# Attention, experts and soft experts on one core: operand sums on VectorE, and expert 0's second products one group later

## The chip, the cores and the metric

One core of a Trainium2 chip. The time is device time in microseconds of one execution. The engines are TensorE (PE in the rows; its weight loads are PEld), VectorE (DVE), ScalarE (ACT), GpSimd (POOL) and SyncE (SP), whose queue issues most DMAs.

## The reference

```python
# attention over q, k, v (4 batches, 8 heads, 576 positions, 64 wide), causal window of 128, ALiBi bias
scores = np.where(mask, scores + bias, -1e9)
attn = softmax(scores); attn_out = attn @ v
x = attn_out.transpose(0, 2, 1, 3).reshape(2304, 512)
# dense mixture: all 4 experts on all tokens, weighted by probabilities
for e in range(4):
    h = np.maximum(x @ w1[e], 0.0)          # 512 -> 1024
    out += p[:, e:e+1] * (h @ w2[e])        # 1024 -> 512
# soft mixture: 8 experts of 4 slots, on softmax-weighted sums of all tokens
logits = out @ phi
slot_input = softmax_over_tokens(logits).T @ out
slot_out[e] = np.maximum(slot_input[e] @ m1[e], 0.0) @ m2[e]
result = softmax_over_slots(logits) @ slot_out
```

## The kernel before

Every product is made in 16-bit parts: an operand is split in a high and a low half (`hi`, `lo`), and three products of halves are added in PSUM. Tokens come in 18 tiles of 128.

**Attention with expert 0 between (up to some 285 us).** The loop in lines 436 to 483 goes over 72 steps, four a tile, each for a pair of heads. Step n makes the scores (`qk`, lines 322 to 336), the softmax (`soft`, lines 338 to 362: VectorE adds the bias and finds the extreme, ScalarE takes exp and the high half, GpSimd the low half at line 358, and a transposing DMA of SP's queue, line 293, makes `eT`), and then the product with v (`pv`, lines 364 to 376) of an earlier step: `LAG` = 2 steps back (line 419; one step for the first tile). `eT` has five buffers (line 360). After a tile's four `pv`, `xn` and `xn_c` normalise it and transpose it to `xT`.

Between the steps, pieces of expert 0 are put in with a budget of 2000 estimated ns a step (line 476). A group is one tile of tokens for the first four, then two. Its pieces (`moe_pieces`, lines 243 to 257) are eight first products (`l1_piece`, L206, one for each 128 columns of the hidden layer, then ScalarE's relu at L214 and VectorE's low half at L215) and after them, for each tile, two halves of the second product (`l2_mm`, L228), the second of which ends with VectorE's L236. First products use two PSUM banks, second products two others. A hidden tile `h` holds two blocks of up to 512 tokens in one of 23 slabs that `acc`, the weights, staged loads and `ct` share. Pieces that the budget leaves over come after the loop (lines 667 to 675), with the jobs of the next stage between.

**Seven-product stage (some 346 to 751 us).** Experts 1, 2 and half of 3 are worked off in 10 quarters (`QS`), each with three groups of six tiles, 30 units. The first products of a unit (`unit_l1`, matmuls at L566) are seven products of sums of operands in place of eight plain ones; the second products (`unit_l2`, L641) of the unit before stand between them, with VectorE's L238 adding each to `acc`. The sums of x are made once for each of the three groups by `xsum_jobs` (lines 500 to 538): eight 128x768 sums at L507 on GpSimd, then ScalarE's L510 and VectorE's L511 for the halves of four results. The sums of weights are made for each quarter by `w7_jobs` (lines 540 to 558): four 128x256 sums at L550 on GpSimd, then L554 and L555. The temporaries of both and the units' `h` share three buffers (`h6`). All three groups' x sums are made ahead of the stage.

**Then** the rest of expert 3, with the soft mixture, and the output.

The code's order sets priorities only: the program is built with a scheduler that goes by a simulated timeline (`schedule_with_timeline_sim=True`), and that may put an instruction which is ready ahead of ones that stand before it. What it fixed is the order on each engine, which the trace shows.

Of the kernel before, what the change touches and what calls it, by code (L numbers as in the profile page):

```python
# [9 lines left out]
F16 = mybir.dt.float16  # L10
BF16 = mybir.dt.bfloat16
AF = mybir.ActivationFunctionType
ALU = mybir.AluOpType
# [6 lines left out]
def kernel(  # L20
# [13 lines left out]
    nc = tc.nc  # L34
    P = 128
# [6 lines left out]
    FC = F // P  # L42
# [27 lines left out]
    def sl(shape, dt, name, pool=None):  # L70
        return (pool or slab).tile(shape, dt, tag="slab", name=nm(name))
# [129 lines left out]
    def l1_piece(e, t0, n, fc, key):  # L201
        pt = ps.tile([P, 512], F32, tag="L1", name=nm("l1"))[:, 0:n]
        first_mm = True
        for kc in range(KC):
            for wa, xa in ((0, 0), (0, 1), (1, 0)):
                nc.tensor.matmul(pt, lhsT=w1_ap(e, fc, wa, kc), rhs=x_ap(t0, n, xa, kc),  # L206
                                 start=first_mm, stop=(kc == KC - 1 and wa == 1))
                first_mm = False
        kk = (key, fc // 2)
        if kk not in hh:  # L210
            hh[kk] = sl([P, 2, 2, 512], F16, "h") if e < 3 else h3[h3n[0] % 2].rearrange("p (a b c) -> p a b c", a=2, b=2)
            h3n[0] += e == 3
        ht = hh[kk][:, fc % 2, :, 0:n]
        nc.scalar.activation(out=ht[:, 0], in_=pt, func=AF.Relu)  # L214
        nc.vector.scalar_tensor_tensor(out=ht[:, 1], in0=pt, scalar=0.0, in1=ht[:, 0],  # L215
                                       op0=ALU.max, op1=ALU.subtract)
# [4 lines left out]
    def l2_mm(e, t, o, fcs, key, lo, hi):  # L221
        if lo == 0:
            l2p[key, t] = ps2.tile([P, 512], F32, tag="L2", name=nm("l2"))
        pt = l2p[key, t]
        for fc in fcs[lo:hi]:
            ht = hh[key, fc // 2]
            for ha, wa in ((0, 0), (0, 1), (1, 0)):
                nc.tensor.matmul(pt, lhsT=ht[:, fc % 2, ha, o:o + P], rhs=w2_ap(e, fc, wa),  # L228
                                 start=(fc == fcs[0] and ha == 0 and wa == 0),
                                 stop=(fc == fcs[-1] and ha == 1))  # L230

# [106 lines left out]
    def soft(i, hp, st):  # L338
# [18 lines left out]
        nc.scalar.activation(out=e2[:, :, 0], in_=et[:, :, c0:], func=AF.Copy)  # L357
        nc.gpsimd.tensor_tensor(out=e2[:, :, 1], in0=et[:, :, c0:], in1=e2[:, :, 0], op=ALU.subtract)  # L358
        nb = 4 * w // P
        eTt = at([P, 8, P], F16, "eT", 5)  # L360
        trans(eTt[:, 0:nb], e2.rearrange("p a b c -> p (a b c)"), nb, i < 2)
        eT[i, hp] = eTt

# [52 lines left out]
    swap_q(0)  # L416
    sp_v_hi(0)
    sp_v_lo(0)
    LAG = 2
    NS = NT * 4  # L420
    PE_T = 2

# [8 lines left out]
    for tl in groups0:  # L431
        avail.append((pvt(4 * tl[-1] + 3) + (3 if tl[-1] else 1), tl))
    pend = []
    wq = [(0, qd, j) for a in (0, 2) for qd in range(4) for j in (a, a + 1)]
    budget = 0.0
    for n in range(NS + LAG + 3):
# [35 lines left out]
        while avail and avail[0][0] <= n:  # L472
            tl = avail.pop(0)[1]
            alloc_acc(tl[0])
            pend += moe_pieces(0, tl, list(range(FC)), True)
        budget = min(budget + 2000.0, 5000.0)
        while pend and budget > 0:
            c, f = pend.pop(0)
# [21 lines left out]
    def xsum_jobs(sg):  # L500
# [3 lines left out]
            return st[i // 2][:, i % 2].rearrange("p k (i t) -> p k i t", t=P)  # L504

        def tt(o, x, y, op):
            nc.gpsimd.tensor_tensor(out=o, in0=x, in1=y, op=op)  # L507

        def out(b, i):
            nc.scalar.activation(out=XS[sg][:, b, 0], in_=st[i // 2][:, i % 2], func=AF.Copy)  # L510
# [29 lines left out]
    def w7_jobs(e, qd):  # L540
        t = {}

        def j0():
            W7[e, qd] = sub.tile([P, 7, 2, 2, P], F16, tag="w7", name=nm("w7"), bufs=2)
            t[0] = h6([P, 4, 2, P], F32, "wt")
            sa = stg[e, qd, 0].rearrange("p (b k) (z f) -> p b k z f", b=2, z=2)
            t[1] = sa
            for o, x, y in ((t[0][:, 0], sa[:, 0, :, 1], sa[:, 0, :, 0]), (t[0][:, 1], sa[:, 1, :, 1], t[0][:, 0]),
                            (t[0][:, 2], sa[:, 1, :, 1], sa[:, 0, :, 1]), (t[0][:, 3], sa[:, 1, :, 0], t[0][:, 1])):
                nc.gpsimd.tensor_tensor(out=o, in0=x, in1=y, op=ALU.subtract)  # L550

        def sp(a, b, src):
            d = W7[e, qd]
            nc.scalar.activation(out=d[:, a:b, 0], in_=src, func=AF.Copy, scale=WS)  # L554
            nc.vector.scalar_tensor_tensor(out=d[:, a:b, 1], in0=src, scalar=WS, in1=d[:, a:b, 0],  # L555
                                           op0=ALU.mult, op1=ALU.subtract)
        return [j0, lambda: sp(0, 2, t[1][:, :, :, 0]), lambda: sp(2, 3, t[1][:, 1:2, :, 1]),
                lambda: sp(3, 7, t[0])]
# [88 lines left out]
    while avail:  # L647
        tl = avail.pop(0)[1]
        alloc_acc(tl[0])
        pend += moe_pieces(0, tl, list(range(FC)), True)  # L650
    QS = [(e, qd) for e in (1, 2) for qd in range(4)] + [(3, 0), (3, 1)]
    QP = [(3, 2), (3, 3)]
    QA = QS + QP
# [1 line left out]
    def qjobs(x):  # L655
# [8 lines left out]
                r += [lambda j=j: split_w(e, qd, j) for j in (0, 1)]  # L664
            r += [lambda j=j: split_w(e, qd, j) for j in (2, 3)]
        return r
    jobs = [lambda: load_w(*QA[0])] + qjobs(0) + [j for sg in range(NSG) for j in xsum_jobs(sg)]
    per = -(-len(jobs) // max(1, len(pend)))
    while pend:
        for _ in range(per):  # L670
# [2 lines left out]
        pend.pop(0)[1]()  # L673
    for jb in jobs:
        jb()
    hh.clear()


    prev = []
    for x, (e, qd) in enumerate(QS):  # L680
        jobs = qjobs(x + 1) + (qjobs(x + 2) if x == len(QS) - 1 else [])
        for sg in range(NSG):
            u, L = unit_l1(e, qd, sg)
            order = [L[0], 0, L[1], L[2], 0, L[3], L[4], 0, 0, L[5], 0, L[6], 0]
# [9 lines left out]
            jb()  # L694
    for f in prev:
        f()
    sums_pool.__exit__(None, None, None)
    slb = ctx.enter_context(tc.tile_pool(name="slb", bufs=17))

# [337 lines left out]
```

## Time and profile before

| | us |
|---|---|
| runs (3), median | 954.52 |
| lowest, highest | 953.16, 954.74 |
| profiled execution | 952.59 |
| its span, first to last instruction | 950.8 |
| TensorE busy in the span | 883.7 |
| VectorE, ScalarE, GpSimd busy | 559.0, 372.4, 269.7 |

The profile is of one execution. A row of grouped instructions names the line, the engine, the operation, the tiles (written <- read), the shape, the count, the busy time in us and the mean of one in ns. A row of waits reads: engine and line that waited <- what ended the wait: us in total, how many times, the longest. PEclk is the granted share of TensorE's clock: 1.00 is 2.4 GHz, 0.50 is 1.2 GHz. Waits of PE and PEld for the same thing overlap and are not to be added.

### The profile page before, as it was taken

The numbers are of one execution on the slowest core, as the hardware profiler recorded it, in microseconds if no ns is written. First come the engines' busy times: TensorE is split into PE (matmuls) and PEld (weight loads), VectorE is DVE, ScalarE is ACT, GpSimd is POOL, SyncE is SP. The second block draws the span as 40 slices with busy tenths as digits, with TensorE's granted clock in tenths as the row PEclk, the third lists the DMA queues.
The fourth block names the chain that finished last, engine by engine and source line by source line (L and its number), as shares of the span: only waits on it lengthen the run. The fifth ranks groups of instructions, "written<-read, shape, count | busy, mean of one in ns | idle before, by whom it ended". The sixth has DMA issues, their size and how long they took to land.

```text
span 950.8 us, 16499 instructions
## 1 busy us (share of the span) xinstructions
PE 883.7 (93%) x6514; PEld 514.7 (54%) x6514; DVE 559.0 (59%) x1170; ACT 372.4 (39%) x920; POOL 269.7 (28%) x240
## 2 busy tenths in 40 slices
PE   3589999899899989999999999999999999999797
PEld 2467766566675545555555555555555445554432
DVE  9965545546538586666565747566657464456612
ACT  5787647767633343323232313232323101222412
POOL 7766536556528940101010110101010004410000
PEclk9999999999999999999999999999999999999799
DMA  9599988999870110100001010101001007983796
GB/s 262 113 184 178 204 142 151 176 187 193 138 148 22 45 45 1 45 15 30 23 23 45 1 45 1 45 1 45 18 28 45 1 1 291 223 217 116 240 385 235
DMA packets 222030, 102.37 MB, mean 108 GB/s; under 512 B 187216, under 2 KB 201584, under 8 KB 221952
## 3 DMA queue, kind: packets, MB, share of 16 engines
q1 hardware_dynamic: 212320, 78.14, 39.1%
q10 hardware_dynamic: 6800, 13.11, 3.9%
q0 software_dynamic: 2832, 10.07, 2.9%
q8 instruction: 51, 0.84, 0.4%
q14 instruction: 27, 0.22, 0.1%
HBM read 64.59 MB, written 4.72 MB: 73 GB/s over the span
## 4 chain that ended last, share of the span: by engine, by line
PE 71%; DMA 9%; POOL 6%; ACT 5%; DVE 4%; issue 3%; SPq 2%; POOLq 0%; ACTq 0%; DVEq 0%
PE l L641 25%; PE A L566 12%; PE l L228 8%; PE l L206 8%; PE C L566 6%; DMA eT<-e 4%; PE B L566 3%; POOL st L507 3%; DMA kT<-ks 2%; DMA qT<-qs 2%; PE hp L969 2%; ACT e L352 1%; PE so_ps L987 1%; PE x L375 1%; PE fp L1000 1%
## 5 line engine op out<-in xcount | busy, mean ns | idle before, releaser
L641 PE MATMUL l<-w,h 128*128 128x512 f16 x1080 | 253.0, 379 | 0.0
L238 DVE SCALAR_TENSOR_TENSOR acc<-l,pr,acc 128x512 f32<-128x512 f32 x216 | 161.5, 749 | 134.2 <-PE l L641 110.8
L566 PEld LDWEIGHTS <-w 128*128 128x128 f16 x1260 | 123.6, 98 | 100.1 <-issue 3.5
L228 PE MATMUL l<-w,h 128*128 128x512 f16 x648 | 161.5, 382 | 8.1 <-ACT h L214 7.0
L641 PEld LDWEIGHTS <-h 128*128 128x128 f16 x1080 | 105.7, 98 | 115.2
L206 PE MATMUL l<-xT,w 128*128 128x256 f16 (+2 forms) x1344 | 162.9, 272 | 4.7 <-DVE h L215 3.9
L206 PEld LDWEIGHTS <-w 128*128 128x128 f16 x1344 | 116.8, 99 | 42.1 <-issue 6.5
L590 ACT ACTIVATE ct<-A 128x384 f32<-128x384 f32 x90 | 43.5, 488 | 219.4 <-PE A L566 219.3
L550 POOL TENSOR_TENSOR wt<-stg 128x256 f32<-128x256 f32 x20 | 14.5, 746 | 336.7 <-PE l L641 297.3
L358 POOL TENSOR_TENSOR e<-e,e 128x512 f16<-128x512 f32 (+1 forms) x72 | 80.7, 1125 | 69.8 <-ACT e L357 49.6
L228 PEld LDWEIGHTS <-h 128*128 128x128 f16 x648 | 60.2, 99 | 63.9 <-ACT h L214 7.8
L214 ACT ACTIVATE h<-l 128x256 f16<-128x256 f32 (+2 forms) x112 | 40.2, 366 | 104.5 <-PE l L206 67.2
L352 ACT ACTIVATE e<-e,nmx 128x256 f32<-128x256 f32 (+1 forms) x144 | 69.7, 485 | 24.6 <-DVE nmx L347 24.4
L215 DVE SCALAR_TENSOR_TENSOR h<-l,h 128x256 f16<-128x256 f32 (+2 forms) x112 | 44.9, 409 | 51.0 <-ACT h L214 50.2
L566 PE MATMUL C<-xs,w 128*128 128x384 f16 x360 | 72.2, 326 | 0.0
L566 PE MATMUL A<-xs,w 128*128 128x384 f16 x360 | 70.7, 329 | 1.0 <-ACT ct L590 1.0
L347 DVE CUSTOM_DVE_ANT_0 e<-s,bias 128x256 f32<-128x256 f32 (+1 forms) x144 | 52.8, 404 | 26.2 <-PE s L335 14.7
L566 PE MATMUL A<-xT,w 128*128 128x384 f16 x360 | 67.6, 326 | 0.6 <-ACT ct L590 0.6
L585 ACT ACTIVATE h<-ct 128x384 f16<-128x384 f32 x90 | 44.0, 515 | 43.8 <-PE l L641 31.6
L593 DVE TENSOR_TENSOR ct<-ct,C 128x384 f32<-128x384 f32 x60 | 33.1, 551 | 36.1 <-ACT ct L590 26.1
L375 PE MATMUL x<-vv,eT 128*128 128x64 f16 x816 | 40.0, 197 | 14.7 <-DMA eT<-e 10.1
L330 PE MATMUL s<-kT,qT 128*128 128x128 f16 x272 | 46.3, 230 | 6.9 <-DVE qT L299 2.5
(181 smaller groups left out, 1040.9 us busy)
## 6 DMA issues: line engine op xcount, KB each, us to landing
m<-in_moe_w_dram ACTq DMA_DIRECT2D x25, 512.0 KB, 5.3
stg<-in_moe_w_dram SPq DMA_DIRECT2D x20, 512.0 KB, 4.6
m<-in_moe_w_dram SPq DMA_DIRECT2D x20, 512.0 KB, 10.2
m<-in_moe_w_dram POOLq DMA_DIRECT2D x19, 512.0 KB, 11.8
stg<-in_moe_w_dram SPq DMA_DIRECT2D x24, 256.0 KB, 3.2
out_dram<-ots SPq DMA_DIRECT2D x18, 256.0 KB, 3.4
qr<-in_q_dram SPq DMA_DIRECT2D x16, 256.0 KB, 4.5
kr<-in_k_dram SPq DMA_DIRECT2D x16, 256.0 KB, 4.0
```

The costliest lines, as they stand in the source:

```text
L206: nc.tensor.matmul(pt, lhsT=w1_ap(e, fc, wa, kc), rhs=x_ap(t0, n, xa, kc), start=first_mm, stop=(kc == KC - 1 and wa == 1))
L215: nc.vector.scalar_tensor_tensor(out=ht[:, 1], in0=pt, scalar=0.0, in1=ht[:, 0], op0=ALU.max, op1=ALU.subtract)
L228: nc.tensor.matmul(pt, lhsT=ht[:, fc % 2, ha, o:o + P], rhs=w2_ap(e, fc, wa), start=(fc == fcs[0] and ha == 0 and wa == 0), stop=(fc == fc ...
L238: nc.vector.scalar_tensor_tensor(out=a, in0=pt, scalar=p, in1=a, op0=ALU.mult, op1=ALU.add)
L330: nc.tensor.matmul(o, lhsT=qT[i][:, 0, h], rhs=mv, start=True, stop=False)
L347: nc.vector.tensor_tensor_reduce(out=et[:, hl, c0:], in0=st[:, hl, c0:], in1=bias[:, h, c0:], op0=ALU.add, op1=ALU.min, scale=-0.125, scal ...
L352: nc.scalar.activation(out=et[:, hl, c0:], in_=et[:, hl, c0:], func=AF.Exp, scale=-1.0, bias=nmx[i][:, h:h + 1], accum_out=sums[i][:, h:h ...
L358: nc.gpsimd.tensor_tensor(out=e2[:, :, 1], in0=et[:, :, c0:], in1=e2[:, :, 0], op=ALU.subtract)
L375: nc.tensor.matmul(o, lhsT=t[:, (hl * 2 + ea) * nk + kb - kb0], rhs=vvs[i - 1 + kb][:, h, va], start=(kb == kb0 and ea == 0 and va == 0), ...
L566: nc.tensor.matmul(o, lhsT=wq_[:, blk, wa, kc], rhs=xf(xa, kc), start=(first and kc == 0 and wa == 0 and xa == 0), stop=(kc == 1 and wa == 1),
L585: nc.scalar.activation(out=o[:, 0], in_=src, func=AF.Relu)
L641: nc.tensor.matmul(pt, lhsT=u["h"][:, z, ha, par, i * P:(i + 1) * P], rhs=w2_ap(e, 2 * qd + z, wa), start=(z == 0 and ha == 0 and wa == 0) ...
```

## The change

It does five things. The x sums (L507) and the weight sums (L550) are issued on VectorE instead of GpSimd. The third group's x sums move from ahead of the seven-product stage into its first quarter, and the first group's come before the first quarter's weight jobs. Expert 0's second products of one group are queued between the first products of the next (`queue_moe0`), the last group's last three pieces between the first products of the stage's first unit (`tail0`). Expert 0's hidden tiles hold four blocks of 256 tokens instead of two of 512. `LAG` goes from 2 to 3 and `eT` from five buffers to six.

```diff
--- before.py
+++ after.py
@@ -206,11 +206,17 @@
                 nc.tensor.matmul(pt, lhsT=w1_ap(e, fc, wa, kc), rhs=x_ap(t0, n, xa, kc),
                                  start=first_mm, stop=(kc == KC - 1 and wa == 1))
                 first_mm = False
-        kk = (key, fc // 2)
-        if kk not in hh:
-            hh[kk] = sl([P, 2, 2, 512], F16, "h") if e < 3 else h3[h3n[0] % 2].rearrange("p (a b c) -> p a b c", a=2, b=2)
-            h3n[0] += e == 3
-        ht = hh[kk][:, fc % 2, :, 0:n]
+        if e == 0:
+            kk = (key, fc // 4)
+            if kk not in hh:
+                hh[kk] = sl([P, 4, 2, 256], F16, "h")
+            ht = hh[kk][:, fc % 4, :, 0:n]
+        else:
+            kk = (key, fc // 2)
+            if kk not in hh:
+                hh[kk] = h3[h3n[0] % 2].rearrange("p (a b c) -> p a b c", a=2, b=2)
+                h3n[0] += 1
+            ht = hh[kk][:, fc % 2, :, 0:n]
         nc.scalar.activation(out=ht[:, 0], in_=pt, func=AF.Relu)
         nc.vector.scalar_tensor_tensor(out=ht[:, 1], in0=pt, scalar=0.0, in1=ht[:, 0],
                                        op0=ALU.max, op1=ALU.subtract)
@@ -223,9 +229,9 @@
             l2p[key, t] = ps2.tile([P, 512], F32, tag="L2", name=nm("l2"))
         pt = l2p[key, t]
         for fc in fcs[lo:hi]:
-            ht = hh[key, fc // 2]
+            ht = hh[key, fc // 4][:, fc % 4] if e == 0 else hh[key, fc // 2][:, fc % 2]
             for ha, wa in ((0, 0), (0, 1), (1, 0)):
-                nc.tensor.matmul(pt, lhsT=ht[:, fc % 2, ha, o:o + P], rhs=w2_ap(e, fc, wa),
+                nc.tensor.matmul(pt, lhsT=ht[:, ha, o:o + P], rhs=w2_ap(e, fc, wa),
                                  start=(fc == fcs[0] and ha == 0 and wa == 0),
                                  stop=(fc == fcs[-1] and ha == 1))
 
@@ -357,7 +363,7 @@
         nc.scalar.activation(out=e2[:, :, 0], in_=et[:, :, c0:], func=AF.Copy)
         nc.gpsimd.tensor_tensor(out=e2[:, :, 1], in0=et[:, :, c0:], in1=e2[:, :, 0], op=ALU.subtract)
         nb = 4 * w // P
-        eTt = at([P, 8, P], F16, "eT", 5)
+        eTt = at([P, 8, P], F16, "eT", 6)
         trans(eTt[:, 0:nb], e2.rearrange("p a b c -> p (a b c)"), nb, i < 2)
         eT[i, hp] = eTt
 
@@ -416,7 +422,7 @@
     swap_q(0)
     sp_v_hi(0)
     sp_v_lo(0)
-    LAG = 2
+    LAG = 3
     NS = NT * 4
     PE_T = 2
 
@@ -431,6 +437,19 @@
     for tl in groups0:
         avail.append((pvt(4 * tl[-1] + 3) + (3 if tl[-1] else 1), tl))
     pend = []
+    late = []
+
+    def queue_moe0(tl):
+        pcs = moe_pieces(0, tl, list(range(FC)), True)
+        l1, l2 = pcs[:FC], pcs[FC:]
+        per_l2 = max(1, len(l1) // max(1, len(late)))
+        for n, pc in enumerate(l1):
+            pend.append(pc)
+            if late and (n + 1) % per_l2 == 0:
+                pend.append(late.pop(0))
+        pend.extend(late)
+        late[:] = l2
+
     wq = [(0, qd, j) for a in (0, 2) for qd in range(4) for j in (a, a + 1)]
     budget = 0.0
     for n in range(NS + LAG + 3):
@@ -472,7 +491,7 @@
         while avail and avail[0][0] <= n:
             tl = avail.pop(0)[1]
             alloc_acc(tl[0])
-            pend += moe_pieces(0, tl, list(range(FC)), True)
+            queue_moe0(tl)
         budget = min(budget + 2000.0, 5000.0)
         while pend and budget > 0:
             c, f = pend.pop(0)
@@ -504,7 +523,7 @@
             return st[i // 2][:, i % 2].rearrange("p k (i t) -> p k i t", t=P)
 
         def tt(o, x, y, op):
-            nc.gpsimd.tensor_tensor(out=o, in0=x, in1=y, op=op)
+            nc.vector.tensor_tensor(out=o, in0=x, in1=y, op=op)
 
         def out(b, i):
             nc.scalar.activation(out=XS[sg][:, b, 0], in_=st[i // 2][:, i % 2], func=AF.Copy)
@@ -547,7 +566,7 @@
             t[1] = sa
             for o, x, y in ((t[0][:, 0], sa[:, 0, :, 1], sa[:, 0, :, 0]), (t[0][:, 1], sa[:, 1, :, 1], t[0][:, 0]),
                             (t[0][:, 2], sa[:, 1, :, 1], sa[:, 0, :, 1]), (t[0][:, 3], sa[:, 1, :, 0], t[0][:, 1])):
-                nc.gpsimd.tensor_tensor(out=o, in0=x, in1=y, op=ALU.subtract)
+                nc.vector.tensor_tensor(out=o, in0=x, in1=y, op=ALU.subtract)
 
         def sp(a, b, src):
             d = W7[e, qd]
@@ -647,7 +666,9 @@
     while avail:
         tl = avail.pop(0)[1]
         alloc_acc(tl[0])
-        pend += moe_pieces(0, tl, list(range(FC)), True)
+        queue_moe0(tl)
+    pend += late[:-3]
+    tail0 = [f for c, f in late[-3:]]
     QS = [(e, qd) for e in (1, 2) for qd in range(4)] + [(3, 0), (3, 1)]
     QP = [(3, 2), (3, 3)]
     QA = QS + QP
@@ -664,7 +685,8 @@
                 r += [lambda j=j: split_w(e, qd, j) for j in (0, 1)]
             r += [lambda j=j: split_w(e, qd, j) for j in (2, 3)]
         return r
-    jobs = [lambda: load_w(*QA[0])] + qjobs(0) + [j for sg in range(NSG) for j in xsum_jobs(sg)]
+    jobs = [lambda: load_w(*QA[0])] + xsum_jobs(0) + qjobs(0) + xsum_jobs(1)
+    jobs0 = xsum_jobs(2)
     per = -(-len(jobs) // max(1, len(pend)))
     while pend:
         for _ in range(per):
@@ -673,12 +695,11 @@
         pend.pop(0)[1]()
     for jb in jobs:
         jb()
-    hh.clear()
-
-
-    prev = []
+
+
+    prev = tail0
     for x, (e, qd) in enumerate(QS):
-        jobs = qjobs(x + 1) + (qjobs(x + 2) if x == len(QS) - 1 else [])
+        jobs = (jobs0 if x == 0 else []) + qjobs(x + 1) + (qjobs(x + 2) if x == len(QS) - 1 else [])
         for sg in range(NSG):
             u, L = unit_l1(e, qd, sg)
             order = [L[0], 0, L[1], L[2], 0, L[3], L[4], 0, 0, L[5], 0, L[6], 0]
@@ -694,6 +715,7 @@
             jb()
     for f in prev:
         f()
+    hh.clear()
     sums_pool.__exit__(None, None, None)
     slb = ctx.enter_context(tc.tile_pool(name="slb", bufs=17))
```

## Rows read from the trace of the kernel before

**Rows 1.** The page, part 1: busy time, share of the span, instructions

```profile
PE 883.7 (93%) x6514; PEld 514.7 (54%) x6514; DVE 559.0 (59%) x1170; ACT 372.4 (39%) x920; POOL 269.7 (28%) x240
```

**Rows 2.** Busy us of each engine by stretch, then PEclk, DMA share, GB/s

```profile
71.00:143.00 72.00, 67.40 (x858) 51.04 (x855) 36.06 (x126) 42.35 (x128) 36.11 (x31) 0.98 1.07 174
143.00:214.00 71.00, 63.11 (x684) 44.76 (x681) 38.46 (x135) 50.02 (x148) 43.32 (x38) 1.00 0.98 172
214.00:285.00 71.00, 67.28 (x734) 48.36 (x732) 37.86 (x120) 41.82 (x120) 34.02 (x29) 1.00 0.91 160
285.00:346.00 61.00, 53.42 (x327) 32.51 (x325) 42.97 (x43) 21.02 (x40) 55.86 (x32) 0.94 0.09 27
346.00:751.00 405.00, 405.00 (x2175) 212.64 (x2174) 249.25 (x413) 121.16 (x254) 24.45 (x34) 1.00 0.09 27
```

**Rows 3.** Waits of PE and of PEld from 55 to 282 us

```profile
PE x L375 <- DMA eT<-e: 10.1, 9, 2.2
PE l L206 <- DVE h L215: 2.0, 2, 1.1
...
PEld L375 <- DMA eT<-e: 13.3, 13, 2.4
PEld L228 <- ACT h L214: 5.8, 3, 2.5
```

**Rows 4.** Waits of PE from 282 to 346 us

```profile
PE B L566 <- DVE ct L593: 2.5, 1, 2.5
PE l L206 <- DVE h L215: 1.9, 3, 0.7
PE A L566 <- ACT ct L590: 1.6, 2, 1.0
PE l L228 <- ACT h L214: 1.3, 1, 1.3
```

**Rows 5.** Chain that ended last, 258 to 352 us, shares by line

```profile
by line: POOL st L507 28.0%; PE l L206 13.2%; PE l L228 12.6%; DVE w L555 7.3%; DVE xs L511 5.9%; PE A L566 5.3%; issue 4.8%; DMA eT<-e 3.5%; DVE w L170 3.2%; PE B L566 2.7%; PE x L375 2.4%; DVE acc L236 2.2%; PE C L566 2.1%; DVE h L215 1.2
```

**Rows 6.** Groups of instructions; L511's row: min/median/max in ns

```profile
L507 POOL TENSOR_TENSOR st<-xT 128x768 f32<-128x768 f16 x12 | 23.8, 1999 | 2.7 <-DVE w L555 2.4
L550 POOL TENSOR_TENSOR wt<-stg,wt 128x256 f32<-128x256 f32 x20 | 15.7, 784 | 0.7
L511 DVE TENSOR_TENSOR xs<-st,xs x12: 946/1733/2560, 299.1 to 342.0; 128x768 f16<-128x768 f32 x12
L593 DVE TENSOR_TENSOR ct<-ct,C 128x384 f32<-128x384 f32 x60 | 33.1, 551 | 36.1 <-ACT ct L590 26.1 <-PE C L566 9.8
L215 DVE SCALAR_TENSOR_TENSOR h<-l,h 128x256 f16<-128x256 f32 x68 | 28.0, 418 | 30.3 <-ACT h L214 29.9
```

**Rows 7.** Two stretches as in rows 2, those at half clock

```profile
314.48:317.89 3.41, 3.41 (x15) 2.00 (x14) 1.52 (x2) 1.23 (x2) 3.41 (x3) 0.50 0.02 5
341.78:345.20 3.42, 3.06 (x10) 1.18 (x9) 2.40 (x2) 1.26 (x4) 3.08 (x4) 0.50 0.00 0
```

**Rows 8.** Timeline of PE: start us, us, instructions in a row

```profile
290.54 0.81 PE L566 MATMUL A<-xT,w 128*128 128x384 f16 x4
...
329.87 3.19 PE L228 MATMUL l<-w,h 128*128 128x512 f16 x14
332.89 1.14 PE L566 MATMUL B<-xT,w 128*128 128x384 f16 x6
```

**Rows 9.** Wait of SP's queue, 55 to 282 us; the eT transposes (min/median/max ns)

```profile
SPq L293 <- POOL e L358: 40.5, 35, 2.9
...
L293 SPq DMA_TRANSPOSE eT<-e x64: 1216/1279/3012, 53.6 to 273.1; - x64
```

**Rows 10.** A quarter of the seven-product stage as in rows 2; waits, 350 to 751 us

```profile
409.30:453.10 43.80, 43.80 (x238) 23.10 (x236) 27.43 (x47) 13.95 (x30) 2.82 (x4) 1.00 0.08 25
...
POOL wt L550 <- PE l L641: 297.3, 7, 47.3
...
DVE acc L238 <- PE l L641: 97.8, 96, 3.6
```

## The prediction

> **What bounds the kernel now.** I read the page's share of each engine first: TensorE is busy for 93% of the span [rows 1]. That mean hides stages, so the next view is the busy time in stretches cut by stage [rows 2]. From 346 to 751 us, the seven-product stage, TensorE is busy for all of its 405 us at full clock, and no matmul of that stretch shows a wait: nothing can be gained there, only lost. From 71 to 285 us (attention with expert 0 between) and from 285 to 346 us (the rest of expert 0, the first operand sums) it isn't full. So the third view is what TensorE waited for in these two [rows 3, 4], and the fourth the chain of work over the second, where the sums on GpSimd hold 28.0% [rows 5]. TensorE is thus the bound from 71 us on at the latest, its work is the same after the change, and the time can move only by what it waits, by its clock, and by new waits. I add up those.
>
> **Operand sums from GpSimd to VectorE.** 24 sums of 128x768 move. On GpSimd the form that reads xT takes 1999 ns mean [rows 6]; on VectorE the nearest row is the subtraction of the same shape, L511, 946 ns where nothing disturbs it, 1733 ns median. All twelve L511 run in the stretch where GpSimd is busy 55.86 of 61 us [rows 2], so I read the median as disturbed by it and take the minimum: 24 x 0.95 = 22.8 us on VectorE for about 48 us on GpSimd. What it frees on the path: the first seven-product matmuls waited 2.5 us for VectorE's ct and 1.6 us for ScalarE's [rows 4], 4.1 us; both queues were then behind slow sums. I take 4.0, bounds 0 and 4.1. VectorE is busy 42.97 of 61 us there [rows 2]; the new 16 sums ahead of the stage (15.2 us) come in while L511 gets shorter (8 or more of them at 0.95 in place of 1.73: 6 us less), so it is about 52 of 61: full, but not the bound. If the median were VectorE's own price, the 16 would take 27.7 us, VectorE would need 42.97 + 27.7 = 70.7 us in a stretch of 61, and the 4.1 us would turn into a loss of about 10; that is a reason for the width of the range.
> The Trainium skill (GPSIMD Engine Reference, Key points) says that GpSimd shares its SBUF interfaces with VectorE and contends with instructions of two SBUF inputs. By that rule the 1733 ns are contention and end with GpSimd's sums, which is the sum as it stands; without it the loss just named would be due.
>
> **The clock in that stretch.** Two stretches of 3.41 us were granted 0.50, that is 1.2 GHz [rows 7]. Each stands behind waits of TensorE: the 1.3 us for ScalarE's h and, just before 341.8 us, the 2.5 us for ct [rows 4]. At half clock 3.41 us do the work of 1.7, so they cost at most 3.4 us together. If the waits go, most of it goes: I take 2.5, bounds 0 and 3.4.
>
> **Second products interleaved, one group later.** Before, the last matmuls L228 of a group wait for the h just made: 5.8 us between 55 and 282 us and 1.3 after it [rows 3, 4], 7.1 us. After it they read an h made a whole group before. I take 6.0, bounds 0 and 7.1. The matmuls L206 wait for VectorE's h to free their two banks, 2.0 + 1.9 = 3.9 us; two L206 pieces and then an L228 piece give that bank more time, but VectorE gets fuller. I take 2.0, bounds -2 (worse by that) and 3.9.
> The price: the first group's second product has no cover until the second group comes. That is 24 matmuls at 0.216 us (14 of them took 332.89 - 329.87 = 3.02 us, rows 8), 5.2 us. But the order on the engine isn't that of the code: product A of the first unit ran at 290.54 us, while expert 0's L228 still ran at 329.87 [rows 8]. Work that is ready is pulled forward, so most of the 5.2 us should still fill early idle time. I take a cost of 1.5, bounds 0 and 5.2. The hidden tiles of four blocks take half of the slabs and move no work. The three pieces carried into the first unit are the same matmuls elsewhere; the first unit has no second products of its own to put between, so they cost nothing, unless the slabs that they hold delay the next load from SP's queue, which has 40 us to come.
>
> **Attention lag 3, six eT buffers.** A PV matmul waits for its transposing DMA: 10.1 us in TensorE's rows and 13.3 in those of its weight loads, two views of mostly the same waits [rows 3]; the longest is 2.4 us. The 64 eT leave between 53.6 and 273.1 us [rows 9], a step every 3.5 us, so one more step of lag covers the longest. Against it: the transposes leave from SP's queue, which itself waits 40.5 us for GpSimd's e [rows 9], and neither e, its buffers nor that queue changes; and if matmuls are pulled forward, PV may be as well, and the lag isn't used. Bounds 0 and 13.3; between ends so far apart I take half, 6.5. The sixth buffer keeps the DMA as free as before, at no time.
>
> **Third group's sums in the first quarter.** 8 sums and 4 subtractions at 0.95 are 11.4 us of VectorE in a stage that has no slack on TensorE. A quarter lasts 43.8 us and VectorE is busy 27.43 of it [rows 10]: 16.4 idle, and VectorE there waits for TensorE (97.8 us for second products in the stage), not the other way round. The first unit also has two additions to acc in place of six. So it is hidden, but in bursts, within two units (29 us). I take 2.0, bounds 0 and 11.4.
>
> **Weight sums, every quarter.** 40 sums of 128x256, 784 ns on GpSimd. On VectorE the nearest rows are 0.418 (L215, 256 columns of another operation) and 0.551 (L593, the same operation, 384 columns) [rows 6]; I take the one of the same size. Four are 1.7 us a quarter, 27.43 + 1.7 = 29.1 of 43.8. Nine quarters come to 15 us if they were all exposed. On GpSimd the first of them waited for the L641 that frees its buffer, 297.3 us in 7 times [rows 10], at no cost as nothing stood behind it; on VectorE the additions to acc and the ct sums queue behind that wait, and TensorE behind these. But the buffer comes free with the last L641 of the unit before, just the matmul whose sum VectorE waits for next in any case. I take 1.0 in all, bounds 0 and 15.
>
> **Sum.** Gains 4.0 + 2.5 + 6.0 + 2.0 + 6.5 = 21.0; costs 1.5 + 2.0 + 1.0 = 4.5; net -16.5 us. The profiled execution took 952.59 us, 950.8 of it in the span: 936.1. The median of the runs is 954.52, 1.9 us (0.2%) above it; I give the forecast on the median's scale, 938.0.
>
> **Rivals.**
> (a) Only the transition gets better. PV waits and L228 waits stay, since the engine's order isn't the code's and SP's queue sets when eT lands. Gains 4.0 + 2.5 + 1.0, costs 4.5: 951.5. For it: the pulled-forward order [rows 8] and SP's waits [rows 9]. Against it: the waits come at few places (3 for L228), where the h is the newest one.
> (b) All named waits and the two half-clock stretches go and nothing is paid: 4.1 + 3.4 + 7.1 + 3.9 + 13.3 = 31.8, 922.7. Against it: an engine order made anew makes some new waits.
> (c) VectorE becomes the pace of the seven-product stage, and the kernel is slower. Place: the first three units and the four sums at the head of each quarter; price 11.4 + 15 = 26.4 us if each burst holds TensorE as long as it lasts, against 21.0 gained: 954.5 - 21.0 + 1.5 + 26.4 = 961.4. It decides once more than about 19.5 of these 26.4 us are exposed. For it: TensorE has no slack there, and a wait for the buffer now stands in VectorE's queue. The Trainium skill (TensorE: Matmul & The Clock Gate, Architectural detail) calls VectorE's queue a strict FIFO, so what stands behind the wait can't pass it; no run here shows that yet, as VectorE had no such wait. Against it: 16.4 us of idle VectorE a quarter.
> (d) The change does nothing net: the gains of (a) and the first group's 5.2 us plus some of the first quarter's burst cancel: 7.5 - 5.2 - 2.0 = 0.3 us, 954.2.
>
> **How the numbers follow.** Forecast 0.52, (a) 0.20, (b) 0.10, (c) 0.12, (d) 0.06. A measurement of this kernel tells a change from none at about 0.2%, 1.9 us. Faster by more than that: forecast, (a) and (b), 0.82; within it (d), 0.06; slower (c), 0.12. The range reaches over (a) and towards (b): 924 to 952. Left out are (c), most of (d) and somewhat under half of (b), about 0.2.
>
> **What would show it.** Right: no TensorE wait for DVE ct or ACT ct at the transition; GpSimd idle from there on; L511 near 0.95 us; L228 not waiting for ACT h; full clock from the last attention step to 751 us; the first unit's product B, at 332.89 us before [rows 8], at about 308 to 316 (the gain, and the carried 7.8 us of second products behind it). PV waits for eT of about half. Wrong: matmuls L566 or L641 with waits on VectorE in the first quarter (c), a gap on TensorE between 50 and 65 us where the first second product was (the 5.2 us), or PV waits as long as before (a).

## The result, and where the time went

The changed kernel took 942.5 us (median of 4 runs, 940.48 to 943.86) against 953.84 for the one before beside it: a ratio of 0.9881, interval 0.9858 to 0.9904, so 11.3 us faster. The profiled execution took 942.66 us, 940.9 of it in the span, 9.9 us less than the span before. In the changed kernel L220 and L221 are the relu and the low half of expert 0's h (L214 and L215 before), L234 its second product (L228), L381 the product with v (L375), L526 the x sums (L507), L530 the subtraction behind them (L511), L569 the weight sums (L550), L585 and L660 the two products of the seven-product stage (L566 and L641), L244 the additions of its second products to acc (L238), L336 the scores (L330).

Waits of TensorE and of its weight loads in attention, 48 to 274 us of the changed kernel, in the form of [rows 3]:

```profile
PE l L206 <- DVE h L221: 8.1, 6, 2.4
PE x L381 <- DMA eT<-e: 7.3, 6, 2.4
PE l L206 <- DMA xT<-xs: 3.5, 2, 2.0
PE s L336 <- DVE nmx L353: 2.6, 1, 2.6
...
PEld L381 <- DMA eT<-e: 9.1, 8, 2.6
```

The waits of expert 0's second product for the new h (5.8 us in [rows 3]) have no row any more. The waits of PV, the product with v, for eT fell from 10.1 to 7.3 us. But L206's waits for VectorE's h rose from 2.0 to 8.1, and waits for xT (3.5) and, through nmx, for the scores' bank (2.6) stand beside them. From 274 to 346 us TensorE has no row of waits at all, where [rows 4] shows four before. Busy time by stretch, as in [rows 2]:

```profile
71.00:143.00 72.00, 64.38 (x854) 50.21 (x853) 40.16 (x134) 46.63 (x139) 39.54 (x34) 0.98 1.11 183
143.00:214.00 71.00, 61.69 (x639) 43.84 (x635) 40.48 (x131) 47.26 (x140) 41.28 (x37) 0.95 1.03 176
214.00:274.00 60.00, 58.89 (x685) 43.77 (x685) 35.49 (x113) 40.13 (x114) 30.80 (x27) 1.00 0.84 141
274.00:336.00 62.00, 62.00 (x399) 38.80 (x397) 41.49 (x65) 18.24 (x37) 0.49 (x1) 1.00 0.19 56
336.00:741.00 405.00, 405.00 (x2175) 212.67 (x2174) 267.26 (x458) 123.93 (x258) 1.51 (x2) 1.00 0.09 27
```

From 274 us on TensorE is busy without a gap and at full clock (1.00), where the kernel before, from 285 to 346 us, had 53.42 of 61 us and 0.94; GpSimd falls from 55.86 us there to 0.49. The chain of work at the transition, which GpSimd's sums led with 28.0% in [rows 5] (258 to 352 us), is now, from 274 to 346 us, TensorE alone:

```profile
by line: PE l L234 44.4%; PE l L206 29.1%; PE A L585 12.4%; PE C L585 5.4%; PE B L585 5.4%; PE l L660 3.6%
```

The moved sums, each line's minimum/median/maximum in ns, in the form of L511's row in [rows 6]:

```profile
L526 DVE TENSOR_TENSOR st<-xT x12: 944/948/959, 278.0 to 341.1; 128x768 f32<-128x768 f16 x12
L526 DVE TENSOR_TENSOR st<-st,st x9: 947/948/948, 282.6 to 344.2; 128x768 f32<-128x768 f32 x9
...
L530 DVE TENSOR_TENSOR xs<-st,xs x12: 944/947/957, 286.2 to 349.2; 128x768 f16<-128x768 f32 x12
...
L569 DVE TENSOR_TENSOR wt<-stg x20: 411/415/419, 281.6 to 689.8; 128x256 f32<-128x256 f32 x20
```

And the end of the stage's last first product, before (first line) and after (second):

```profile
L566 PE MATMUL C<-xs,w x360: 326/326/326, 304.4 to 751.0; 128*128 128x384 f16 x180
```

```profile
L585 PE MATMUL C<-xs,w x360: 325/326/327, 296.7 to 740.9; 128*128 128x384 f16 x180
```

The last of them starts 10.1 us earlier, and the whole span is 9.9 us shorter: all of the gain lies ahead of the stage's end, none behind it.

To compare kernels I worked out one number for each stretch: the distance between the starts of consecutive matmuls, less the columns of the first at 2.4 GHz, summed. It is the time that TensorE lost in the stretch to waits, low clock and short matmuls; its work is the same in every kernel here. The boundaries are the same for all. The loss is that of the one profiled execution, the median that of all runs.

| lost by TensorE, us | 0 to 48 | 48 to 274 | 274 to 350 | 350 to 741 | median, us | ratio to before |
|---|---|---|---|---|---|---|
| before | 32.2 | 42.6 | 13.3 | 5.2 | | 1 |
| changed | 31.6 | 45.4 | 1.2 | 5.2 | 942.5 | 0.9881 (0.9858 to 0.9904) |
| sums only | 32.1 | 42.6 | 4.8 | 5.2 | 943.55 | 0.9914 (0.9891 to 0.9938) |
| interleaving only | 31.6 | 48.4 | 9.2 | 5.2 | 952.26 | 0.9996 (0.9978 to 1.0013) |
| lag only | 31.5 | 45.4 | 10.9 | 5.2 | 952.0 | 0.9991 (0.9973 to 1.001) |
| changed, no lag | 32.2 | 47.1 | 1.2 | 5.2 | 944.39 | 0.9921 (0.99 to 0.9943) |
| changed, third group ahead | 31.6 | 46.0 | 2.2 | 5.2 | 944.38 | 0.9912 (0.9895 to 0.993) |
| changed, sums on GpSimd | 31.6 | 44.3 | 6.2 | 5.2 | 947.98 | 0.9947 (0.9928 to 0.9966) |
| changed, weight sums four times | 31.6 | 47.1 | 1.2 | 6.6 | 944.3 | 0.9905 (0.9887 to 0.9924) |
| changed, single tiles plain | 32.2 | 40.8 | 1.2 | 5.2 | 938.73 | 0.9852 (0.9829 to 0.9874) |
| changed, two ks | 31.4 | 42.9 | 1.2 | 5.2 | 938.45 | 0.984 (0.9821 to 0.9858) |
| single tiles plain, two ks | 31.6 | 40.0 | 1.2 | 5.2 | 935.59 | 0.9809 (0.9789 to 0.9829) |
| same with two qs, five eT | 32.5 | 42.0 | 1.2 | 5.2 | 938.84 | 0.9839 (0.9821 to 0.9857) |
| sums, lag, two ks, plain throughout | 31.5 | 47.0 | 4.8 | 5.2 | 943.93 | 0.9892 (0.9869 to 0.9915) |

The changed kernel gained 12.1 us between 274 and 350 us and gave 2.8 back in attention. Each kernel was timed beside the kernel before on its own chip; ratios are what is compared.

How far one execution can be trusted, four rows of the table show. The changed kernel and the ones with the third group ahead, with sums on GpSimd and with weight sums four times have the same order of TensorE's instructions up to 274 us, and lost 45.4, 46.0, 44.3 and 47.1 us in attention; half clock (0.50) was granted there for 10.2, 13.7, 3.4 and 13.7 us. So differences of up to some 3 us in that column are scatter between executions. All four lie above the 42.6 us of the kernel before and of sums only, whose order there is the same too: that attention got worse is borne out, by 1.7 to 4.5 us. The column of the transition is steadier: of the kernels with the interleaving and the sums on VectorE, all but the one with the third group ahead lost 1.2 us there.

### The profile page after: what moved, and what is told of

Read it like the earlier page. It is cut to its first block, busy times and chain, and to the rows that moved or that the text cites. A ratio compares the mean times of both kernels' runs of the same rounds, so it can differ in the third digit from the quotient of the medians.

```text
span 940.9 us, 16481 instructions
## 1 busy us (share of the span) xinstructions
PE 877.4 (93%) x6514; PEld 512.3 (54%) x6514; DVE 577.1 (61%) x1234; ACT 372.6 (40%) x920; POOL 189.3 (20%) x176
## 4 chain that ended last, share of the span: by engine, by line
PE 76%; DMA 7%; issue 5%; ACT 4%; POOL 3%; DVE 3%; SPq 2%; POOLq 0%; ACTq 0%; DVEq 0%
PE l L660 22%; PE A L585 12%; PE l L206 11%; PE l L234 10%; PE C L585 6%; PE B L585 3%; ACT e L358 2%; PE hp L991 2%; DMA qT<-qs 2%; PE x L381 2%; PE so_ps L1009 2%; DMA m<-in_moe_w_dram 1%; PE s L341 1%; DMA eT<-e 1%; PE fp L1022 1%
## 5 line engine op out<-in xcount | busy, mean ns | idle before, releaser
L660 PE MATMUL l<-w,h 128*128 128x512 f16 x1080 | 252.8, 379 | 0.0
L244 DVE SCALAR_TENSOR_TENSOR acc<-l,pr,acc 128x512 f32<-128x512 f32 x216 | 161.4, 748 | 127.1 <-PE l L660 103.3
L585 PEld LDWEIGHTS <-w 128*128 128x128 f16 x1260 | 123.3, 98 | 94.0
L206 PE MATMUL l<-xT,w 128*128 128x256 f16 (+2 forms) x1344 | 160.5, 271 | 12.6 <-DVE h L221 8.1
L660 PEld LDWEIGHTS <-h 128*128 128x128 f16 x1080 | 105.7, 98 | 115.2
L234 PE MATMUL l<-w,h 128*128 128x512 f16 x648 | 153.1, 381 | 0.7 <-DVE acc L244 0.7
L206 PEld LDWEIGHTS <-w 128*128 128x128 f16 x1344 | 115.9, 99 | 46.2 <-issue 10.1
L754 POOL DMA_DIRECT2D m<-in_moe_w_dram x19 | 13.8, 725 | 510.1 <-DVE h L605 446.9
L234 PEld LDWEIGHTS <-h 128*128 128x128 f16 x648 | 61.9, 98 | 64.4 <-issue 2.6
L221 DVE SCALAR_TENSOR_TENSOR h<-l,h 128x256 f16<-128x256 f32 (+2 forms) x112 | 45.0, 409 | 62.5 <-ACT h L220 62.1
L220 ACT ACTIVATE h<-l 128x256 f16<-128x256 f32 (+2 forms) x112 | 40.2, 365 | 106.5 <-PE l L206 69.3
L585 PE MATMUL C<-xs,w 128*128 128x384 f16 x360 | 71.2, 326 | 0.0
L585 PE MATMUL A<-xs,w 128*128 128x384 f16 x360 | 69.3, 326 | 0.0
L585 PE MATMUL A<-xT,w 128*128 128x384 f16 x360 | 67.6, 326 | 0.0
L604 ACT ACTIVATE h<-ct 128x384 f16<-128x384 f32 x90 | 43.8, 515 | 46.5 <-PE l L660 25.1
L336 PE MATMUL s<-kT,qT 128*128 128x128 f16 x272 | 44.9, 228 | 9.3 <-DVE nmx L353 5.1
L381 PE MATMUL x<-vv,eT 128*128 128x64 f16 x816 | 39.3, 197 | 11.5 <-DMA eT<-e 7.3
L605 DVE SCALAR_TENSOR_TENSOR h<-ct,h 128x384 f16<-128x384 f32 x90 | 47.6, 550 | 2.3 <-ACT h L604 2.1
## 6 DMA issues: line engine op xcount, KB each, us to landing
m<-in_moe_w_dram SPq DMA_DIRECT2D x20, 512.0 KB, 10.2
```

The costliest lines, as they stand in the source:

```text
L234: nc.tensor.matmul(pt, lhsT=ht[:, ha, o:o + P], rhs=w2_ap(e, fc, wa), start=(fc == fcs[0] and ha == 0 and wa == 0), stop=(fc == fcs[-1] an ...
L244: nc.vector.scalar_tensor_tensor(out=a, in0=pt, scalar=p, in1=a, op0=ALU.mult, op1=ALU.add)
L336: nc.tensor.matmul(o, lhsT=qT[i][:, 0, h], rhs=mv, start=True, stop=False)
L381: nc.tensor.matmul(o, lhsT=t[:, (hl * 2 + ea) * nk + kb - kb0], rhs=vvs[i - 1 + kb][:, h, va], start=(kb == kb0 and ea == 0 and va == 0), ...
L585: nc.tensor.matmul(o, lhsT=wq_[:, blk, wa, kc], rhs=xf(xa, kc), start=(first and kc == 0 and wa == 0 and xa == 0), stop=(kc == 1 and wa == 1),
L605: nc.vector.scalar_tensor_tensor(out=o[:, 1], in0=src, scalar=0.0, in1=o[:, 0], op0=ALU.max, op1=ALU.subtract)
```

## The experiments

The theory after the two traces, T: the whole gain is the end of the waits and of half clock between 282 and 350 us, the sums bring it, and the parts in attention cancel. The rival P is the prediction's own split, in which interleaving and lag bring 6.5 us each.

### Each part alone

**Sums only.** The kernel before with the sums on VectorE and the third group's in the first quarter.

```diff
-            nc.gpsimd.tensor_tensor(out=o, in0=x, in1=y, op=op)
+            nc.vector.tensor_tensor(out=o, in0=x, in1=y, op=op)
...
-                nc.gpsimd.tensor_tensor(out=o, in0=x, in1=y, op=ALU.subtract)
+                nc.vector.tensor_tensor(out=o, in0=x, in1=y, op=ALU.subtract)
...
-    jobs = [lambda: load_w(*QA[0])] + qjobs(0) + [j for sg in range(NSG) for j in xsum_jobs(sg)]
+    jobs = [lambda: load_w(*QA[0])] + xsum_jobs(0) + qjobs(0) + xsum_jobs(1)
+    jobs0 = xsum_jobs(2)
...
-        jobs = qjobs(x + 1) + (qjobs(x + 2) if x == len(QS) - 1 else [])
+        jobs = (jobs0 if x == 0 else []) + qjobs(x + 1) + (qjobs(x + 2) if x == len(QS) - 1 else [])
```

> The kernel before with one part of the change: operand sums and weight sums on VectorE, third group's sums in the first quarter. Theory T (the whole gain is the end of waits and half clock between 282 and 350 us, and the parts in attention cancel): 9 to 12 us faster, about 943 to 945, as the changed kernel; TensorE's waits for DVE ct and ACT ct and both half-clock stretches gone there, its waits in attention as before (eT 10, ACT h 5). Rival P (the terms as they were predicted): 4.0 + 2.5 + part of the L206 wait - 3.0, some 4 us faster, 950.

Measured: 943.55 us, ratio 0.9914 (0.9891 to 0.9938), some 8 us faster. TensorE's waits from 282 to 350 us:

```profile
PE l L206 <- DVE h L215: 0.9, 1, 0.9
PE C L566 <- DVE xs L511: 0.9, 1, 0.9
PE A L566 <- ACT ct L590: 0.6, 1, 0.6
PE A L566 <- DVE w L555: 0.2, 1, 0.2
```

The 2.5 us for ct is gone and no wait is longer than 0.9 us; attention lost 42.6 us as before. The stretch is at full clock (1.00). That is T's mechanism, a little under T's 9 to 12 us, and twice what P gave it. But the sums don't bring the whole gain at the transition: TensorE lost 8.5 us less there (13.3 to 4.8) and not 12.1. By ratio the changed kernel is some 3 us better than this one, and the two intervals overlap.

**Interleaving only.** The change's `queue_moe0`, `tail0` and hidden tiles; sums, lag and eT as before.

```diff
-            pend += moe_pieces(0, tl, list(range(FC)), True)
+            queue_moe0(tl)
```

> The kernel before with the second products of expert 0 one group later, its hidden tiles of four blocks and the three carried pieces; sums on GpSimd ahead of the stage, lag 2, five eT buffers. Theory T: L228's waits for ACT h (7 us) go, but L206's waits for VectorE's h grow from 4 to about 9 us, since the group's own second products no longer fill in; net within 3 us of before, and the transition still waits for GpSimd's sums (up to 10 us). Rival P: 6.0 + 2.0 - 1.5 = 6.5 us faster, 947.

**Lag only.** The kernel before with

```diff
-    LAG = 2
+    LAG = 3
...
-        eTt = at([P, 8, P], F16, "eT", 5)
+        eTt = at([P, 8, P], F16, "eT", 6)
```

> The kernel before with lag 3 and six eT buffers alone. Theory T: PV's waits for eT shrink by a third at most (12.7 to 8.5 us between both traces), and what is won is lost to other waits in attention: within 3 us of before. Rival P: 6.5 us faster, 947.

Measured: 952.26 us (0.9996) and 952.0 us (0.9991), both no change. TensorE's waits from 48 to 282 us, interleaving only:

```profile
PE x L381 <- DMA eT<-e: 13.6, 16, 2.7
PE l L206 <- DVE h L221: 4.3, 4, 1.9
```

and lag only:

```profile
PE x L375 <- DMA eT<-e: 9.6, 7, 2.7
PE l L228 <- ACT h L214: 5.4, 3, 2.5
PE l L206 <- DVE h L215: 4.2, 5, 2.1
```

Interleaving takes the second products' waits for h (L228 before, L234 here) away in attention, and PV's waits for eT grow from 10.1 to 13.6 us. The lag shortens PV's waits by little (10.1 to 9.6), and L206's double from 2.0 to 4.2. In both, what one wait gives another takes, and no gain is left in the time: P falls for these two terms. At the transition both lost less (9.2 and 10.9 us, after 13.3), and in attention more.

**The changed kernel without the lag** (`LAG = 2`, five eT buffers).

> The changed kernel with lag 2 and five eT buffers again. Theory T: the lag brings nothing, so this stays within 2 us of the changed kernel, 941 to 945. Rival P: 6.5 us slower than the changed kernel, 949.

Measured: 944.39 us, 0.9921 (0.99 to 0.9943) beside 0.9881 of the changed kernel: 1.9 us slower by the medians, as T had it, but 3.8 by the ratios, on which the kernels are compared. The intervals just overlap; a worth of the lag of up to some 4 us on top of the interleaving isn't excluded. PV's wait is 10.4 us there:

```profile
PE x L381 <- DMA eT<-e: 10.4, 16, 2.7
```

### Engine or place of the sums

**Third group ahead of the stage again**, on VectorE.

```diff
-    jobs = [lambda: load_w(*QA[0])] + xsum_jobs(0) + qjobs(0) + xsum_jobs(1)
-    jobs0 = xsum_jobs(2)
+    jobs = [lambda: load_w(*QA[0])] + xsum_jobs(0) + qjobs(0) + xsum_jobs(1) + xsum_jobs(2)
+    jobs0 = []
```

> The changed kernel with the third group's x sums ahead of the stage again (on VectorE). If the engine is what counts: VectorE has 20 us idle between 274 and 336 us and these are 11.4, so it stays within 2 us of the changed kernel, 941 to 945. If the place is what counts: the first units wait behind them and 4 us or more of the gain are lost, 946 or above.

**All sums on GpSimd again**, the third group's in the first quarter: the first two edits of "sums only" taken back in the changed kernel.

> The changed kernel with all sums on GpSimd again, the third group's still in the first quarter. If the engine is what counts: 16 sums of 2 us are 32 us of GpSimd ahead of the stage and slow VectorE's subtractions to 1.7 us, the waits for ct come back, 3 to 7 us slower than the changed kernel, 946 to 950. If the place is what counts: as the changed kernel, 941 to 945.

Measured: 944.38 us (0.9912) with the third group ahead, 947.98 us (0.9947, 0.9928 to 0.9966) on GpSimd. The engine counts: on GpSimd the interval lies apart from the changed kernel's, and 6.2 us are lost at the transition where it loses 1.2. The place of the third group isn't shown to count on VectorE: its interval overlaps, with 2.2 us lost. On GpSimd it may: interleaving only, with all sums ahead and lag 2, lost 9.2 us there, and no run tells place and lag apart. TensorE's wait from 282 to 350 us isn't for ct any more, as was expected, but for the h of expert 0's last pieces, which in VectorE's queue stands behind slow subtractions (L530) and weight splits (L574):

```profile
PE l L206 <- DVE h L221: 4.6, 3, 2.0
```

```profile
L530 DVE TENSOR_TENSOR xs<-st,xs x12: 950/1434/2392, 286.3 to 342.6; 128x768 f16<-128x768 f32 x12
```

Both kernels have that subtraction on VectorE; beside GpSimd's sums its median is 1434 ns, without them 947.

### VectorE's room in the stage

**Weight sums four times over.** Twelve instructions more on VectorE in each of nine quarters, same values.

```diff
-                            (t[0][:, 2], sa[:, 1, :, 1], sa[:, 0, :, 1]), (t[0][:, 3], sa[:, 1, :, 0], t[0][:, 1])):
+                            (t[0][:, 2], sa[:, 1, :, 1], sa[:, 0, :, 1]), (t[0][:, 3], sa[:, 1, :, 0], t[0][:, 1])) * (4 if (e, qd) != QA[0] else 1):
```

> The changed kernel with the four weight sums of each later quarter made four times over (12 more instructions of 0.415 us on VectorE a quarter, same values). If mean idle time decides (VectorE busy 29 of 43.8 us, then 34): no change within 2 us. If the burst decides (16 in a row hold VectorE's queue for 6.6 us, and two banks cover some 3 us of that): 2 to 4 us a quarter in nine quarters, 18 to 36 us slower.

Measured: 944.3 us, 0.9905 (0.9887 to 0.9924), its interval overlapping that of the changed kernel. The groups of these sums, and all that TensorE waited for from 350 to 750 us:

```profile
L569 DVE TENSOR_TENSOR wt<-stg,wt 128x256 f32<-128x256 f32 x74 | 30.7, 415 | 0.3
L569 DVE TENSOR_TENSOR wt<-stg 128x256 f32<-128x256 f32 x74 | 29.7, 416 | 0.0
```

```profile
PE l L660 <- DVE acc L244: 0.8, 1, 0.8
```

These are 148 instructions and 60.4 us of VectorE where the changed kernel has 40 x 0.415 = 16.6. TensorE waited 0.8 us for all of it and lost 1.4 us more in the stage (6.6 against 5.2). Rival (c), a VectorE that becomes the pace, isn't near. The wait for a buffer that (c) feared in VectorE's queue isn't there either: in the changed kernel VectorE never stood idle before L569, where GpSimd had stood 297.3 us [rows 10].

### What attention lost

**Single tiles plain.** In the changed kernel the first group's second product has to wait for the second group's first products. This one keeps the old order for the four groups of one tile.

```diff
         l1, l2 = pcs[:FC], pcs[FC:]
+        if len(tl) == 1:
+            pend.extend(pcs)
+            return
```

> The changed kernel with expert 0's pieces in the old order for the four groups of one tile, one group later only from the first group of two tiles on. If L206's waits for VectorE's h in attention (8.1 us by 6) come from second products that are no longer there to fill early: they fall to 3 to 5 us, L228's for ACT h come back by 1 to 3, and it is 2 to 5 us faster, 938 to 941. If they come from VectorE's own queue: within 2 us of the changed kernel.

Measured: 938.73 us, 0.9852 (0.9829 to 0.9874). TensorE's waits from 48 to 274 us:

```profile
PE x L381 <- DMA eT<-e: 7.4, 9, 2.1
PE l L206 <- DVE h L221: 5.1, 5, 2.4
PE l L234 <- ACT h L220: 4.9, 4, 2.6
PE l L206 <- DMA xT<-xs: 2.2, 1, 2.2
```

L206's waits fall to 5.1 from 8.1 (8.1 to 9.7 in the four executions with the changed kernel's order), L234's for the new h come back with 4.9 (more than the 1 to 3 expected), and TensorE loses 4.6 us less in attention (45.4 to 40.8, below all four). So the second products that were put off were cover for L206's waits. How much of the 4.6 us that is stays open: all waits together fell by 1.9 us (21.5 to 19.6), and this execution had half clock for 2.4 us of attention where the changed kernel had 10.2. The version is faster than the kernel before; over the changed kernel it gains 2.8 us by the ratios, with intervals that overlap.

**Two buffers for ks.** One of the two longest waits of L206 in the changed kernel (2.2 us at 93.9 us; the longest, 2.4 at 140.9, goes back over the DMA for qT) goes back over ScalarE, whose queue stands at the split of the keys for a transposing DMA to free their one buffer. The two rows of the timeline, TensorE's and ScalarE's (start us, us, what, in brackets the idle time before and what ended it):

```profile
93.94 0.83 PE L206 MATMUL l<-xT,w 128*128 128x128 f16 x12 [2.24 <-DVE h L221]
```

```profile
92.77 0.63 ACT L281 ACTIVATE ks<-kr 128x512 f16<-128x512 f32 x1 [2.02 <-DMA kT<-ks]
```

To make room, the scratch of the bias shares a buffer.

```diff
-    scr = at([P, 2 * P], F32, "scr", 1)
+    scr = at([P, 2 * P], F32, "x", 2)
...
-        t = at([P, H, 2, D], F16, nme + "s", 1)
+        t = at([P, H, 2, D], F16, nme + "s", 2 if nme == "k" else 1)
```

> The changed kernel with two buffers for the split keys ks in attention instead of one (the scratch of the bias, used once at the start, shares a buffer of x to make room). In the changed kernel's trace the longest wait of L206 for VectorE's h goes back over ScalarE, whose queue stands 2.0 us at ks L281 for the transposing DMA of the keys to free that buffer, with two relus behind. If that queue is the cause: ScalarE's waits for DMA kT (11.2 us by 8) go to under 3, L206's waits for h (8.1) fall by a third or more, and it is 2 to 4 us faster than the changed kernel, 938 to 941. If it is the order of the pieces alone: within 2 us of it.

> The kernel of e7 (old order for the four groups of one tile) with two buffers for ks. If both causes add: 1 to 4 us faster than e7's 938.7, 935 to 938. If they are the same waits: as e7.

Measured: 938.45 us (0.984) on the changed kernel, 935.59 us (0.9809, 0.9789 to 0.9829) on the one with single tiles plain, the fastest here. ScalarE's waits at the keys were, in the changed kernel,

```profile
ACT qs L281 <- DMA qT<-qs: 12.5, 7, 4.3
ACT ks L281 <- DMA kT<-ks: 11.2, 8, 3.2
```

and the second of these with two ks on the changed kernel (first line) and on the one with single tiles plain (second), which had 10.3 with one buffer:

```profile
ACT ks L281 <- DMA kT<-ks: 1.8, 3, 1.4
ACT ks L281 <- DMA kT<-ks: 5.7, 5, 2.0
```

The waits for qT, whose buffer stayed single, didn't fall (13.0 and 8.9 us, after 12.5 and 8.4). TensorE's waits with two ks on the changed kernel, 48 to 274 us:

```profile
PE x L381 <- DMA eT<-e: 9.5, 5, 3.8
PE l L206 <- DVE h L221: 7.6, 7, 4.3
PE l L206 <- DVE nmx L353: 0.5, 1, 0.5
...
PE l L206 <- DMA xT<-xs: 0.2, 1, 0.2
```

The time came as expected, but not by the row named: L206's waits for h fell by 0.5 us only, to 7.6, one of them 4.3 us long; what went are the waits for xT (3.5 to 0.2) and for the scores' bank (2.6, no row), while PV's for eT rose from 7.3 to 9.5. So the second buffer is worth time, but ScalarE's queue isn't shown to be the cause of L206's waits; that one stays open beyond the part that the single tiles hold. With both edits, in the fastest kernel:

```profile
PE x L381 <- DMA eT<-e: 8.1, 8, 2.3
PE l L206 <- DVE h L221: 3.5, 5, 1.3
...
```

**Two qs as well, five eT buffers.** `nme + "s", 2` for both, `"eT", 5`, lag 3, on the kernel with single tiles plain.

> The kernel of e7 with two buffers for qs and for ks, and five eT buffers instead of six to make room, lag 3 kept. ScalarE's waits for DMA qT (8.4) and kT (10.3) should both go. If they count more than the sixth eT buffer: 2 to 5 us faster than e7, 934 to 937. If the sixth buffer is what lag 3 needs: PV's waits or SP's waits for PV grow and it is as e7 or slower, 939 to 943.

Measured: 938.84 us (0.9839): 3 us slower than the fastest and as fast as single tiles plain. ScalarE's waits at L281 were expected to go; those for qT kept 8.4 us and those for kT 6.2. It has both edits in it, so which of them costs the time isn't told apart.

**Plain order throughout**, with the other parts and two ks.

> The kernel before with sums on VectorE and the third group's in the first quarter, lag 3, six eT buffers and two ks buffers, but expert 0's pieces in the old order throughout and nothing carried into the first unit. Against the same with the interleaving from the two-tile groups on (e9, 935.6). If the interleaving is worth something once the rest is in place: L228's waits for ACT h (6 us) and some 3 us between 274 and 350 us are back, 938 to 944. If it isn't: 934 to 937.

Measured: 943.93 us, 0.9892 (0.9869 to 0.9915), 8 us slower than the fastest. TensorE's waits from 274 to 350 us:

```profile
PE l L206 <- DVE h L215: 1.4, 3, 0.8
PE C L566 <- DVE w L555: 0.7, 1, 0.7
PE A L566 <- ACT ct L590: 0.6, 1, 0.6
```

The 3.6 us that the interleaving is worth between 274 and 350 us (4.8 lost, 1.2 with it) came as expected; the rest is in attention (47.0 against 40.0 us lost in the two profiled executions). Of that, half clock is 7.5 us against 2.9, worked out as the table is, and may be scatter; L228's waits were 1.7 us and not 6. The hidden tiles are the old ones here, two blocks of 512 tokens, so that what the 8 us owe to the order of the pieces and what to the tiles isn't told apart.

## Why the prediction was right, and where its steps were off

The sign and the range held: 11.3 us gained where 16.5 were forecast. The mechanism held for the transition and the stage, and failed for attention, which was to bring the most and brought nothing. The place of the gain is that of rival (a), "only the transition gets better", although L228's waits did go and (a) gave it 3.0 us only. That the time still lay nearer to the forecast (938.0) than to (a) (951.5) was in part luck: more at the transition, no cost in the stage and 0.6 us ahead of 48 us made up for about half of what attention lacked. The steps, by the trace of the changed kernel:

- **The transition** (sums, clock, and the shares of L228 and L206 after 282 us): 4.0 + 2.5 and, shared out by the waits in [rows 3, 4], some 2 were taken, 8.6 in all; TensorE lost 12.1 us less (13.3 to 1.2). Right, and too small: every wait named there went, and so did both half-clock stretches; their bounds, 4.1 + 3.4 + 1.3 + 1.9, come to 10.7, and the rest was in gaps that weren't named. The sums alone bring 8.5 of it. The 946 ns were the right price: 948 measured. VectorE's 52 of 61 us were too many: 41.49 of 62 us were measured, in part because the third group's four slow subtractions left the stretch too and weren't taken off.
- **L228's waits for the new h**, 6.0: they went in full, as said, but interleaving alone left the time as it was (0.9996).
- **L206's waits for its banks**, a gain of 2.0, with -2 as the bad end: the sign was wrong and the bound too near. In attention they grew by 6.1 us (2.0 to 8.1). The step of the prediction that failed is "two L206 pieces and then an L228 piece give that bank more time". The second products that were ready had been what TensorE did while a bank was waited for; put off, they leave the wait open, as the 5.1 us of single tiles plain bear out in part.
- **The first group's second product without cover**, taken at 1.5 of 5.2 because work that is ready is pulled forward: single tiles plain, which takes the new order back for all four groups of one tile, lost 4.6 us less in attention. What of it is the first group's, and what scatter, isn't told apart, so the run shows a price but not that the upper end was right. Why the scheduler didn't pull these forward as it did product A wasn't tried.
- **Lag 3**, taken at 6.5 of 13.3: PV's waits fell by 2.8 us in TensorE's rows and 4.2 in those of its loads, and the lag alone moved nothing. The reason given against it there, that SP's queue and what feeds it don't change, was right: with the lag alone that queue waited 39.7 us for GpSimd's e, after 40.5. Adding up waits as if each went by itself was the error common to these terms: in the runs of single parts, where one wait of TensorE in attention went or shrank, others grew.
- **Half clock in attention** had no term. It was granted for 6.8 us there before and for 10.2 after, but for 3.4 to 13.7 in executions of the same order: what the change does to it isn't shown.
- **The seven-product stage**, 3.0 of cost: none. No wait in either trace, 5.2 us lost in both, and 43.8 us more of VectorE's work cost TensorE 1.4 us. Rival (c) was given 0.12; the 16.4 us of idle VectorE a quarter were the better argument.

By stretch: in attention some 10.9 us were forecast and -2.8 came; at the transition 8.6 and 12.1; in the stage -3.0 and 0.0; 0.6 came ahead of 48 us. The sum is the profiled 9.9. The product B of the first unit, forecast at 308 to 316 us, started at 329.9: attention gave none of its part, and the scheduler put a little more of the seven products ahead of it (30 matmuls of A and C from 295.7 us on, 24 before).

## What to carry to other kernels

Where one engine is full in most stages, add up what it loses by stretch, and trust a gain most where a single queue holds it up (the sums here: 8.5 us by themselves) and least where several queues feed each other: there a wait that ends may come back elsewhere. A change that brings nothing alone (the interleaving with its hidden tiles, 0.9996) can still help together with others: without it the fastest kernel is 8 us slower. Work that is put off to smooth a later step may have been cover for an earlier one; put it off only where other work is there to take its place. And before a difference of one trace is explained, see how far executions with the same order differ (here 3 us in attention).

## What the runs showed of the hardware

GpSimd's sums slow VectorE's instructions of two SBUF inputs by about half and more: the same 128x768 subtraction took 947 ns median with GpSimd quiet and 1434 to 1733 beside it. Within one run, that with the sums on GpSimd, the four subtractions that ran while GpSimd was idle took 950 to 960 ns, and the eight beside its work 1082 to 2392. A 128x768 sum took 948 ns on VectorE and 1812 to 2396 on GpSimd (medians of its forms), a 128x256 one 415 and about 730 to 784.
